# Two spare tiles shift the SBUF addresses of the buffers of a feed-forward stage

## The chip, the cores and the metric

The kernel runs on one core of one Trainium2 chip. The metric is device time in microseconds (us) of one execution, smaller being better. The kernel before takes 998.57 us, the median of three runs between 998.44 and 998.62 us. Nothing but the kernel's program differs between before and after: the inputs, the core and the way of timing are the same.

The engines have short names here: PE is TensorE (matmuls), PEld its loading of weights, DVE is VectorE, ACT is ScalarE, POOL is GpSimd and SP is SyncE, which issues most of the DMAs. SBUF is the on-chip memory, in which a tile has the same address in each of 128 partitions; PSUM is the memory into which matmuls write. All addresses below are bytes within a partition.

## The reference

An input x of 2048 rows by 640 columns goes through two halves. In the first, x is normalized, scaled and convolved along the 2048 rows with a long filter for every column, which the kernel does by its own two-step Fourier transform. In the second, the result is normalized again and goes through a gated feed-forward network of width 1728:

```
h = layernorm(x) * (1 + cb) + sb
gate, up = h @ w1, h @ w3                 # 2048x640 by 640x1728, twice
out = x + gb * ((silu(gate) * up) @ w2)   # 2048x1728 by 1728x640
```

The six row vectors such as cb, sb and gb come from one more small product. All inputs and outputs are 32-bit floats.

## The kernel before, in words

The program has two stages, one after the other on the same core.

**The Fourier stage** takes the time up to some 390 us. Its work is a list of tasks which a planner (the class Plan) puts into one order by written-out ranks; each engine then runs its instructions in just that order (the class InOrder). Its tiles lie in the pools early, gp, tbl and gw, which grow upward from the low end of SBUF, and in xsp, inv and core, which lie against the high end.

**The feed-forward stage** takes the rest. The function change() inside run() (L914) closes the low pools and opens in their place xp, ip and wp; after the plan has been run, run() closes inv and core and opens in their place the pool ffn against the high end (L958). Then ffn() (L755) loops over four blocks b of 512 rows, and within each over 14 slices m of 128 of the 1728 features (the last slice has 64, for gate and up together). One pass of that loop does the following.

- weights_load() (L703) brings the slices of w1, w3 and w2 into the tiles wr and w2r by DMAs of 320 KB. Each is split into a high and a low part, whose sum is the number itself: wh and w2h are copies in the type float32r on ACT (L732, L733), wl and w2l are the differences on DVE (L741, L745).
- up() (L792) multiplies. For each of gate and up, and each of the five blocks k of 128 columns, three matmuls follow one another (L800, L801, L802): high by high, high weights by low activations, low weights by high activations. The weights (128 columns of a tile, 512 bytes in a partition) are loaded into the array; the activations xh or xl (512 columns, 2048 bytes in a partition) move through it. That is 30 matmuls for a full slice.
- gate() (L805) makes the product of silu(gate) and up on ACT and DVE and splits it into ah and al.
- down() (L829) multiplies by w2, again in three matmuls for each of five pieces of the output, 15 in a full slice, all at L837. For pieces k = 0 to 3 the roles are changed: 128 columns of ah or al are loaded as weights and 512 columns of w2h or w2l move. For k = 4, which is done first, w2h or w2l is loaded and ah or al moves, as in up().

The order here is that of the text, with the down() of one slice behind the up() of the next, as the framework's own scheduler arranges it. ln2() (L669) normalizes the next block of 512 rows while the loop runs and writes xh and xl; output() (L839) adds the result to x2 and stores it. During block 0 the last part of the Fourier transform back is still done between the slices (inverse_unit, L660). awake() (L523) puts in a few matmuls of 32-bit floats, with no use of their result, while PE would wait before the first block.

Every matmul of up() and down() works in float32r; all other matmuls (awake, the transposes of ln2 at L691, the Fourier transforms) work in plain 32-bit floats.

The addresses follow from the sizes of the tiles, since a pool puts one tile behind the other. The pool xp begins at 19872, which is 38 times 512 plus 416; nearly all sizes in xp, ip and wp are multiples of 512 (the two small ones, of 480 and 32 bytes, make one together), so that wd, x20, the iz tiles, wr, w2r, wh, w2h, wl and w2l all begin 416 bytes past a multiple of 512. The pool ffn ends at 229344 and begins at 113984, and its tiles xn, xh, xl, v, th, a, ah, al, u, gb, oc and og begin 480 bytes past a multiple of 512; its first three, x21, x22 and x23, begin 320 bytes past one, because five small tiles of 32 bytes follow them. Between the low and the high pools 4512 bytes are free.

Of the kernel before, what the change touches and what calls it, by code (L numbers as in the profile page):

```python
# [10 lines left out]
F32 = mybir.dt.float32  # L11
# [7 lines left out]
P = 128  # L19
# [263 lines left out]
class K:  # L283
# [581 lines left out]
    def run(self):  # L865
# [7 lines left out]
        def open_(name, side=None, bufs=1, space=None):  # L873
            scopes[name] = ExitStack()
            return self.pool(name, bufs=bufs, space=space, ctx=scopes[name], side=side)

        def close(*names):
            for n in names:
                scopes.pop(n).close()
# [34 lines left out]
        def change():  # L914
            close("gw", "tbl", "gp", "early")
            self.xp, self.ip, self.wp = open_("xp"), open_("ip"), open_("wp")
            self.wd = self.xp.tile([P, NJ, 2, 64], F32, name="wd")
            self.x2 = [self.xp.tile([P, 4, D], F32, name="x20")]
            nc.sync.behind = nc.tensor.prev
            self.load_x2(0)  # L920
            nc.sync.dma_start(self.wd, self.t_wd)
            nc.sync.behind = None
            self.stats = self.ln_begin(self.ip, "n0")
        add = plan.add
        add("change", None, 0, change, [f"g{b}.7.p", f"g{b}.7.d"] + [f"h{b}.{i}.x" for i in range(4)], 0)
        add("fx", "SP", 0, None, ["change"], 0, dma=[327680] * 4 + [1048576])
        self.ahead = {}
# [30 lines left out]
        pool = open_("ffn", "right")  # L958
# [20 lines left out]
                nxt[b + 1] = self.ln2(b + 1, pool, ps)  # L979

        self.ffn(nxt, wp, pool, ps, po, mid)
        close("ps", "po", "ffn", "wp", "ip", "xp")

    def mod_cols(self, pm):
# [583 lines left out]
```

## Time and profile before

| what | value |
|---|---|
| median of three timed runs | 998.57 us |
| lowest and highest of them | 998.44 and 998.62 us |
| span of the profiled execution | 994.1 us |
| PE busy in the span | 894.6 us, 90% |
| DVE busy | 665.9 us, 67% |
| ACT busy | 496.7 us, 50% |
| POOL busy | 287.9 us, 29% |

The profile is of one execution. Its span runs from the first to the last instruction; what lies around the span belongs to the execution as well. The profile gives no time of its own for that one execution beside the span; against the median of the timed runs 4.5 us lie around it. Busy time of an engine is the time covered by at least one of its instructions: matmuls overlap in the pipeline, so a PE that is always busy still may be slower or faster at what it does, and the distance from the start of one matmul to the start of the next tells more than the duration of one.

### The profile page before, as it was taken

To read this page: it belongs to the slowest core of one execution; us is meant where nothing else is said; L and a number is where in the kernel's file an instruction comes from. 1 tells how busy PE (TensorE), PEld (TensorE's weight loads), DVE (VectorE), ACT (ScalarE), POOL (GpSimd) and SP (SyncE) were. 2 spreads that over 40 slices of the span, in tenths; PEclk is the share of its full clock that TensorE was granted. 3 is DMA by queue.
4 is the path that set the end of the run, shared out by engine and by line. 5 is a ranking of instruction groups with operands and counts; after the bars stand their busy time and mean duration, and the time that the engine had idled before them with its cause. 6 is when DMAs were issued, how large, how long until landed. Compare 5 with 4: busy or idle time off the path is not lost.

```text
span 994.1 us, 20194 instructions
## 1 busy us (share of the span) xinstructions
PE 894.6 (90%) x8095; PEld 708.9 (71%) x8095; DVE 665.9 (67%) x1235; ACT 496.7 (50%) x829; POOL 287.9 (29%) x293
## 2 busy tenths in 40 slices
PE   1464878889999997999999999999999999999997
PEld 1133766767787863677788888888888888888885
DVE  7998999999999574677564553463644544645443
ACT  6878787979788732432253333343432332433221
POOL 1798798989998330100000000000000000000000
PEclk9986998999999999999999999999999999999999
DMA  9955553614041397996232363332443323543311
GB/s 218 269 184 185 116 135 104 148 52 122 24 108 46 77 272 202 232 233 163 70 90 79 106 162 91 90 98 78 120 132 107 92 80 94 145 119 80 105 28 53
DMA packets 141189, 122.03 MB, mean 123 GB/s; under 512 B 13480, under 2 KB 124840, under 8 KB 139688
## 3 DMA queue, kind: packets, MB, share of 16 engines
q1 hardware_dynamic: 140360, 119.84, 45.8%
q8 instruction: 63, 1.03, 0.5%
q10 hardware_dynamic: 736, 0.92, 0.3%
q14 instruction: 30, 0.25, 0.1%
HBM read 99.75 MB, written 20.97 MB: 121 GB/s over the span
## 4 chain that ended last, share of the span: by engine, by line
PE 72%; DVE 15%; ACT 4%; issue 3%; DMA 3%; POOL 2%; SPq 2%; DVEq 0%; ACTq 0%; POOLq 0%
PE acc L837 19%; PE gu L802 13%; PE gu L801 12%; PE gu L800 12%; PE ps L157 4%; DVE yy L157 3%; PE kps L157 2%; PE fz L157 2%; DVE fp L157 2%; DVE hn L157 2%; PE fk L157 2%; DVE xx L157 2%; PE fh L157 2%; SPq L157 2%; PE iy L652 1%
## 5 line engine op out<-in xcount | busy, mean ns | idle before, releaser
L802 PE MATMUL gu<-xh,wl 128*128 128x512 f32 x540 | 212.9, 394 | 0.0
L801 PE MATMUL gu<-xl,wh 128*128 128x512 f32 x540 | 211.6, 392 | 0.0
L800 PE MATMUL gu<-xh,wh 128*128 128x512 f32 x540 | 210.5, 392 | 0.7 <-ACT xh L666 0.7
L732 ACT ACTIVATE wh<-wr 128x640 fp32r<-128x640 f32 x105 | 71.8, 731 | 136.0 <-PE gu L801 132.8
L744 POOL MEMSET w2l<- 64x640 f32 x3 | 1.9, 628 | 450.6 <-PE acc L837 450.6
L801 PEld LDWEIGHTS gu<-xl,wh 128*128 128x128 f32 x540 | 101.5, 188 | 23.7 <-DVE xl L667 0.2
L800 PEld LDWEIGHTS gu<-xh,wh 128*128 128x128 f32 x540 | 101.4, 188 | 23.2 <-ACT xh L666 1.0
L802 PEld LDWEIGHTS gu<-xh,wl 128*128 128x128 f32 x540 | 101.5, 188 | 21.4
L813 ACT ACTIVATE th<-gu 128x512 f32<-128x512 f32 x52 | 31.1, 599 | 129.8 <-PE gu L802 129.7
L815 DVE TENSOR_TENSOR a<-a,gu 128x512 f32<-128x512 f32 x52 | 35.7, 687 | 87.7 <-PE gu L802 87.5
L157 POOL TENSOR_TENSOR yy<-e,e 128x512 f32<-128x512 f32 x80 | 86.2, 1094 | 17.1 <-PE kps L157 12.2
L814 DVE SCALAR_TENSOR_TENSOR a<-th,gu 128x512 f32<-128x512 f32 x52 | 35.6, 686 | 76.4 <-ACT th L813 76.3
L837 PE MATMUL acc<-w2l,ah 128*128 128x512 f32 x219 | 86.6, 396 | 0.0
L733 ACT ACTIVATE w2h<-w2r 128x640 fp32r<-128x640 f32 x54 | 39.9, 738 | 93.6 <-issue 54.8
L837 PE MATMUL acc<-w2h,ah 128*128 128x512 f32 x219 | 86.6, 395 | 0.0
L741 DVE TENSOR_TENSOR wl<-wr,wh 128x640 fp32r<-128x640 f32 x105 | 82.4, 817 | 0.0
L745 DVE TENSOR_TENSOR w2l<-w2r,w2h 128x640 fp32r<-128x640 f32 (+1 forms) x54 | 44.4, 821 | 56.7 <-ACT w2h L733 56.6
L157 POOL TENSOR_TENSOR ph<-p,p 128x1024 int32<-128x1024 int32 x40 | 80.0, 2000 | 5.2 <-ACT tr L157 5.0
L837 PE MATMUL acc<-w2h,al 128*128 128x512 f32 x203 | 77.2, 395 | 0.0
L157 DVE TENSOR_TENSOR yy<-yy,tr 128x512 f32<-128x512 f32 (+1 forms) x80 | 75.3, 943 | 0.9 <-ACT tr L157 0.6
L157 PE MATMUL kps<-yy,xx 128*32 128x64 f32 x2560 | 53.0, 240 | 24.8 <-DVE xx L157 21.7
L157 PEld LDWEIGHTS kps<-yy,xx 128*32 128x32 f32 x2560 | 46.5, 120 | 34.6 <-issue 17.6
(231 smaller groups left out, 1695.7 us busy)
## 6 DMA issues: line engine op xcount, KB each, us to landing
wr<-in_w SPq DMA_DIRECT2D x104, 320.0 KB, 3.9
w2r<-in_w SPq DMA_DIRECT2D x52, 320.0 KB, 2.9
zd<-zt SPq DMA_DIRECT2D x39, 256.0 KB, 2.8
iz<-zd SPq DMA_DIRECT2D x24, 320.0 KB, 7.2
xs<-in_x SPq DMA_DIRECT2D x16, 320.0 KB, 11.3
hs<-hb SPq DMA_DIRECT2D x20, 256.0 KB, 2.5
xb<-hs SPq DMA_DIRECT2D x20, 256.0 KB, 4.6
x<-in_x SPq DMA_DIRECT2D x16, 320.0 KB, 9.6
```

The lines of the kernel that those rows point to most:

```text
L157: self.prev = self.k.order(f(*a, **kw), self.prev)
L732: self.nc.scalar.activation(wh[:, i], raw[:, i], AF.Copy)
L733: self.nc.scalar.activation(w2h, w2r, AF.Copy)
L741: eng.tensor_tensor(wl[:, i], raw[:, i], wh[:, i].bitcast(F32), op=ALU.subtract)
L745: eng.tensor_tensor(w2l[q], w2r[q], w2h[q].bitcast(F32), op=ALU.subtract)
L800: nc.tensor.matmul(pg, wh[:, k, :], xh[:, k, :], start=(k == 0), stop=False)
L801: nc.tensor.matmul(pg, wh[:, k, :], xl[:, k, :], start=False, stop=False)
L802: nc.tensor.matmul(pg, wl[:, k, :], xh[:, k, :], start=False, stop=(k == KT - 1))
L813: nc.scalar.activation(th, gu[0], AF.Tanh, scale=0.5)
L814: nc.vector.scalar_tensor_tensor(a, th, 1.0, gu[0], op0=ALU.add, op1=ALU.mult)
L815: nc.vector.tensor_mul(a, a, gu[1])
L837: nc.tensor.matmul(acc[k], *two(a, w), start=(m == 0 and i == 0), stop=(m == 12 and i == 2))
```

## The change

Two tiles that no instruction reads or writes are put into two pools.

```diff
         def change():
             close("gw", "tbl", "gp", "early")
             self.xp, self.ip, self.wp = open_("xp"), open_("ip"), open_("wp")
+            self.xp.tile([P, 24], F32, name="pad_left")
             self.wd = self.xp.tile([P, NJ, 2, 64], F32, name="wd")
             self.x2 = [self.xp.tile([P, 4, D], F32, name="x20")]
...
         self.ffn(nxt, wp, pool, ps, po, mid)
+        pool.tile([P, 120], F32, name="pad_right")
         close("ps", "po", "ffn", "wp", "ip", "xp")
```

pad_left has 24 numbers, 96 bytes, and stands first in xp: all that follows in xp, ip and wp begins 96 bytes higher. pad_right has 120 numbers, 480 bytes, and stands last in ffn, a pool whose end is fixed: all else in ffn begins 480 bytes lower. Worked out from the sizes:

| tiles | begin before, past a multiple of 512 | begin after |
|---|---|---|
| wd, x20, iz, wr, w2r, wh, w2h, wl, w2l | 416 | 0 |
| xn, xh, xl, v, th, a, ah, al, u, gb, oc, og | 480 | 0 |
| x21, x22, x23 | 320 | 352 |

The Fourier stage's own tiles stay where they are. No instruction is added, removed or moved in the text of the program.

## The prediction

> **What bounds the kernel now.** I first read the page for the engine that ends last, then the table by stage for the part in which the change lies, then the groups of matmuls, and last the single start times.
>
> ```profile
> span 994.1 us, 20194 instructions
> PE 894.6 (90%) x8095; PEld 708.9 (71%) x8095; DVE 665.9 (67%) x1235; ACT 496.7 (50%) x829; POOL 287.9 (29%) x293
> ...
> PE 72%; DVE 15%; ACT 4%; issue 3%; DMA 3%; POOL 2%; SPq 2%; DVEq 0%; ACTq 0%; POOLq 0%
> PE acc L837 19%; PE gu L802 13%; PE gu L801 12%; PE gu L800 12%; PE ps L157 4%; DVE yy L157 3%; PE kps L157 2%; PE fz L157 2%; DVE fp L157 2%; DVE hn L157 2%; PE fk L157 2%; DVE xx L157 2%; PE fh L157 2%; SPq L157 2%; PE iy L652 1%
> ```
>
> The chain that ended last is PE for 72%, and four lines of the feed-forward stage (L800, L801, L802, L837) are 56% of the span. By stretches of that stage (columns: stretch, its length, then busy us and count of PE, PEld, DVE, ACT and POOL, the granted clock, the share of the DMA engines, GB/s):
>
> ```profile
> 500.00:600.00 100.00, 100.00 (x452) 81.94 (x451) 52.59 (x79) 36.83 (x58) 0.63 (x1) 1.00 0.41 109
> 600.00:700.00 100.00, 100.00 (x446) 81.83 (x445) 48.22 (x70) 35.84 (x55) 0.00 (x0) 1.00 0.33 90
> 700.00:800.00 100.00, 100.00 (x448) 81.77 (x447) 52.82 (x76) 35.34 (x55) 0.63 (x1) 1.00 0.41 111
> 800.00:900.00 100.00, 100.00 (x438) 81.47 (x437) 54.20 (x79) 34.81 (x54) 0.63 (x1) 1.00 0.39 106
> 900.00:980.00 80.00, 80.00 (x349) 65.26 (x348) 33.64 (x48) 22.68 (x35) 0.00 (x0) 1.00 0.24 66
> ```
>
> PE is busy without a gap at full clock; DVE has at most 54%, ACT 37%, the DMA engines 41%. PE's own waits from 400 to 980 us are two:
>
> ```profile
> PE iy L652 <- DVE x L655: 0.4, 1, 0.4
> PE acc L837 <- ACT ah L666: 0.3, 1, 0.3
> ```
>
> So the stage lasts as long as its matmuls do back to back. Faster DMAs, DVE or ACT would buy nothing; the change can act on the end only through the pace of the matmuls.
>
> **What sets that pace.** The groups of the stage (busy us, mean ns of one):
>
> ```profile
> L802 PE MATMUL gu<-xh,wl 128*128 128x512 f32 x540 | 212.9, 394 | 0.0
> L801 PE MATMUL gu<-xl,wh 128*128 128x512 f32 x540 | 211.6, 392 | 0.0
> L800 PE MATMUL gu<-xh,wh 128*128 128x512 f32 x540 | 210.5, 392 | 0.7 <-ACT xh L666 0.7
> L837 PE MATMUL acc<-w2l,ah 128*128 128x512 f32 x219 | 86.6, 396 | 0.0
> L837 PE MATMUL acc<-w2h,ah 128*128 128x512 f32 x219 | 86.6, 395 | 0.0
> L837 PE MATMUL acc<-w2h,al 128*128 128x512 f32 x203 | 77.2, 395 | 0.0
> L837 PE MATMUL acc<-ah,w2h 128*128 128x512 f32 x55 | 22.5, 409 | 0.3 <-ACT ah L666 0.3
> L837 PE MATMUL acc<-ah,w2l 128*128 128x512 f32 x55 | 21.6, 392 | 0.0
> L837 PE MATMUL acc<-al,w2h 128*128 128x512 f32 x51 | 20.3, 398 | 0.0
> ```
>
> In a name the moving operand stands first. That makes 1620 + 161 = 1781 matmuls whose moving operand is a tile of the pool ffn (480 bytes past a multiple of 512) with weights from wp (416), and 641 with the roles changed; eighteen more at the end have another line and are left out. The 392 to 398 ns overlap; the pace is in the start times (start us, duration us):
>
> ```profile
> 652.00 0.39 PE L800 MATMUL gu<-xh,wh 128*128 128x512 f32 x1
> ...
> 664.36 0.39 PE L837 MATMUL acc<-ah,w2h 128*128 128x512 f32 x1
> ...
> 665.05 0.39 PE L837 MATMUL acc<-w2h,ah 128*128 128x512 f32 x1
> ...
> 667.85 0.39 PE L800 MATMUL gu<-xh,wh 128*128 128x512 f32 x1
> ...
> 862.76 0.40 PE L800 MATMUL gu<-xh,wh 128*128 128x512 f32 x1
> ...
> 869.76 0.40 PE L800 MATMUL gu<-xh,wh 128*128 128x512 f32 x1
> ```
>
> 54 matmuls of up() from 652.00 to 664.36 take 12.36 us, 228.9 ns each. The 12 of down() with the roles changed, 665.05 to 667.85, take 233.3 each. There are also stretches of up() at 233.3: 30 from 862.76 to 869.76 in 7.00 us. What would the moving of 512 columns alone cost? The matmuls in plain 32-bit floats tell:
>
> ```profile
> 377.79 7.13 PE L157 MATMUL awake<-wd,ident 128*128 128x512 f32 x16
> ...
> 388.49 2.84 PE L157 MATMUL awake<-wd,ident 128*128 128x512 f32 x6
> ...
> 644.92 1.47 PE L691 MATMUL tp<-ident,xn 128*128 128x128 f32 x12
> ```
>
> ```profile
> L691 PE MATMUL tp<-ident,xn x80: 271/272/329, 394.0 to 793.8; 128*128 128x128 f32 x80
> ```
>
> The row by itself gives min, median and max of one transpose, 271, 272 and 329 ns. The awake groups give (7.13 - 2.84) / 10 = 429 ns from start to start, the transposes (1.47 - 0.27) / 11 = 109 ns. Between 128 and 512 columns that is 0.833 ns a column and 2.4 ns for each instruction, and neither pays anything for its addresses, though wd begins 416 and xn 480 bytes past a multiple of 512. The float32r matmuls take about half as long a column: at 0.417 ns, 512 columns and 2.4 ns would be 215.7. They are 13.2 ns (up) and 17.6 ns (down) over that.
>
> In which steps? Sixteen columns are 64 bytes and take 6.67 ns. 228.9 / 6.67 is 34.3 and 233.3 / 6.67 is 35.0, while 429 / 6.67 is 64.4, which is just its 1024 column times and 2.4 ns. So in the fast type alone the pace falls on whole and third parts of the time for 64 bytes, which speaks for operands that are fetched in pieces of 64 bytes with nothing to spare. All of these operands begin 32 bytes past a multiple of 64. A moving operand of 2048 bytes that begins there touches 33 such pieces instead of 32, a weight tile of 512 bytes 9 instead of 8. And 228.9 against 233.3, with the same shape and the same order of three, goes with which tile moves: k = 4 of down(), whose roles are those of up(), takes (665.05 - 664.36) / 3 = 230. So the place of the operands, or their distance from one another, matters already now.
>
> **The change part by part.** The pads are touched by no instruction: no instruction, DMA or wait is added in the text, and the high and low pools, 4512 bytes apart, still don't meet (96 + 480 bytes). What may change is three things.
>
> First, which old tile lies under a new one, and so which last use the new tile waits for. By the sizes I find the low pools over the same tiles as before, but for the 96 bytes at their start. On the high side x22 and x23 each come free of one tile of the pool inv, four of the small tiles of ln2 lie over another of its output buffers, and og0 over one more tile of core. All of these owners are done before the first inverse product of the second stage, which reads what they stored, and og0 is written only when the first block is done: I take nothing, and both ends of the price are nothing.
>
> Second, DVE, ACT and the DMAs get other addresses. The scaling of ln2 reads x20 (416) in two of its eight DVE instructions and x21 to x23 (320, a multiple of 64) in six:
>
> ```profile
> L680 DVE TENSOR_SCALAR xn<-x,rs_y_n,rs_n_n x8: 605/608/612, 392.9 to 653.1; 128x640 f32<-128x640 f32 x8
> ```
>
> 605 to 612 ns over all eight: no effect of 64 bytes there. That x21 to x23 themselves come to lie 32 bytes past a multiple of 64 should then cost nothing. The DMAs' share has no bearing, since PE waits for none of them from 400 us on; if PE were 6% faster, DVE would rise to 58%, still no bound.
>
> Third, the matmuls. No row here has a float32r operand on a multiple of 64 bytes, so the price is bounded from both sides. Best, all of the excess goes: 1781 x 13.2 ns + 641 x 17.6 ns = 34.8 us. Worst by the rows here, all take the slower pace that is seen: 1781 x 4.4 ns = 7.8 us more. I take one piece of 64 bytes less for each moving operand, 2422 x 6.67 ns = **16.2 us less**. It lies between the bounds and is the row's own step; the other part of the excess would stay with the loading of the weights. All of it is on the path, since PE ends the stage.
>
> [...]
>
> **The rivals.** *All the excess goes*: place was its only cause, and the pace becomes 215.7. For it: plain matmuls show none. Against it: they run at half the pace and may hide anything, the loading of the weights included. 998.6 - 34.8 = 963.8.
>
> *The change does nothing to the pace*: the step is one of time, from the loading of weights beside a moving operand that has no slack, wherever both lie. For it: the same operands of up() run at 228.9 and at 233.3, so history matters. 998.6.
>
> *Slower*: now weights and moving operand begin at the same place within 512 bytes, where they were 64 bytes apart. If the two streams, read at the same time, come to the same part of the memory, up() falls to the pace of down(), and with it everything: 998.6 + 7.8 = 1006.4. It decides as soon as up() loses its 228.9, in the first slice of block 0. For it: turning the distance around, as down() does, costs 4.4 ns already. [...]
>
> *The change doesn't do what it says*: x21 to x23 stay off, but no matmul reads them; the operands of all 2422 do come to multiples of 512.
>
> **How the numbers follow.** The span of the profiled execution is 994.1 us, the median of the timed runs 998.57, and the 4.5 us around the span stay, so that the sum may be taken from the median. One piece less: 998.6 - 16.2 = **982.4 us**, chance 0.38, with an own range of 976 to 991 (1.4 times that to half of it). All gone, 963.8: 0.15. Nothing, 998.6: 0.25. Slower, 1006.4: 0.22. Cases of both signs hold much of the chance, so the range takes both bounds: **963 to 1007**. 0.2% is 2 us, about what a measurement of this kernel can tell from no change: faster 0.53, same 0.25, slower 0.22.
>
> **What would show it.** Up to 390 us the new trace should agree with the old in all its stretches. Then L800 to L802 should start 222 ns apart and the matmuls of down() 227, with mean durations 6 to 7 ns lower in every group above, while the awake matmuls stay at 429, the weight loads stay as they are, and L680 stays within 605 to 612. If the groups move by 13 to 18 ns, all of the excess was place; if up() is at 233, the distance of the two streams is what counts; if neither moves, the step is time alone. I would be wrong altogether if the difference came from before 390 us, from a new wait of PE, or from a clock under 1.00 in the stretches above.

## The result, and the profile after

The changed kernel takes 987.23 us, the median of four runs between 986.33 and 988.79 us; the kernel before takes 998.51 us beside it. The ratio is 0.9887, with an interval of 0.9873 to 0.9901: faster by 11.3 us or 1.1%. The prediction was 982.4, with a range of 963 to 1007. The profiled execution of the changed kernel took 987.09 us, with a span of 985.3, so 1.8 us lie around the span.

The head of the page and its chain of waits, for the changed kernel:

```profile
span 985.3 us, 20196 instructions
PE 884.0 (90%) x8095; PEld 707.7 (72%) x8095; DVE 665.6 (68%) x1235; ACT 496.6 (50%) x829; POOL 287.9 (29%) x293
...
PE 70%; DVE 15%; ACT 4%; DMA 3%; issue 3%; SPq 2%; POOL 2%; DVEq 0%; ACTq 0%; POOLq 0%
PE acc L837 19%; PE gu L800 12%; PE gu L801 12%; PE gu L802 12%; DVE yy L157 3%; PE ps L157 3%; PE kps L157 2%; SPq L157 2%; DVE fp L157 2%; PE fz L157 2%; DVE hn L157 2%; DVE xx L157 2%; PE fk L157 2%; PE fh L157 2%; PE iy L652 1%
```

The same engine and the same four lines carry the end. PE has as many matmuls as before and 10.6 us less busy time; the other engines have what they had. By stretches (the columns are those of the table shown before):

```profile
500.00:600.00 100.00, 100.00 (x457) 83.19 (x456) 54.81 (x82) 38.38 (x60) 0.63 (x1) 1.00 0.39 109
600.00:700.00 100.00, 100.00 (x453) 83.08 (x452) 47.29 (x68) 34.54 (x53) 0.00 (x0) 1.00 0.34 96
700.00:800.00 100.00, 100.00 (x454) 83.04 (x453) 54.82 (x79) 37.22 (x58) 0.63 (x1) 1.00 0.39 109
800.00:900.00 100.00, 100.00 (x444) 82.84 (x443) 52.86 (x78) 33.90 (x53) 0.63 (x1) 1.00 0.40 112
```

PE stays busy without a gap, at the same full clock, and gets more matmuls into the same time: 457, 453, 454 and 444 where there were 452, 446, 448 and 438, 1.3% more. DVE and the DMA engines have as much room as before. The groups of the matmuls (busy us, mean ns of one):

```profile
L800 PE MATMUL gu<-xh,wh 128*128 128x512 f32 x540 | 210.8, 392 | 0.1
L802 PE MATMUL gu<-xh,wl 128*128 128x512 f32 x540 | 210.3, 390 | 0.0
L801 PE MATMUL gu<-xl,wh 128*128 128x512 f32 x540 | 210.3, 390 | 0.0
...
L837 PE MATMUL acc<-w2h,ah 128*128 128x512 f32 x219 | 85.4, 390 | 0.0
L837 PE MATMUL acc<-w2l,ah 128*128 128x512 f32 x219 | 85.4, 390 | 0.0
...
L837 PE MATMUL acc<-w2h,al 128*128 128x512 f32 x203 | 76.1, 390 | 0.0
```

The groups with w2h and w2l moving lose 5 to 6 ns of mean duration, L801 and L802 lose 2 to 4, L800 nothing. The start times say it better (start us, duration us):

```profile
600.75 0.39 PE L800 MATMUL gu<-xh,wh 128*128 128x512 f32 x1
...
607.55 0.39 PE L837 MATMUL acc<-ah,w2h 128*128 128x512 f32 x1
...
608.23 0.39 PE L837 MATMUL acc<-w2h,ah 128*128 128x512 f32 x1
...
610.95 0.39 PE L800 MATMUL gu<-xh,wh 128*128 128x512 f32 x1
```

The 30 matmuls of up() from 600.75 to 607.55 start 226.7 ns apart, and so do the 12 of down() from 608.23 to 610.95. Taken over the whole stage, from start to start where one matmul follows the other directly, the distances are:

| ns from start to start | before | after |
|---|---|---|
| up(), 1606 and 1605 distances | 229.6 | 226.8 |
| down(), k = 4, 152 distances | 229.3 | 227.0 |
| down(), k = 0 to 3, 639 distances | 233.2 | 227.3 |
| all, 2397 and 2396 distances | 230.57 | 226.96 |

The distance is counted for the matmul that it follows. So 3.61 ns for each of some 2400 matmuls, 8.7 us, came from the pace. How long the stage lasts is in the rows of L800, whose first and last start stand behind the durations (min, median, max in ns). The kernel before:

```profile
L800 PE MATMUL gu<-xh,wh x540: 388/388/496, 397.1 to 979.2; 128*128 128x512 f32 x180
```

The changed kernel:

```profile
L800 PE MATMUL gu<-xh,wh x540: 388/389/793, 396.5 to 970.5; 128*128 128x512 f32 x180
```

From the first to the last it was 582.1 us and is 574.0: 8.1 us less. The remaining 3 us of the 11.3 are not in this stage; the last experiments come back to them.

### The profile page after: what moved, and what is told of

The parts are those of the page before. It is cut to its first block, busy times and chain, and to the rows that moved or that the text cites. A ratio compares the mean times of both kernels' runs of the same rounds, so it can differ in the third digit from the quotient of the medians.

```text
span 985.3 us, 20196 instructions
## 1 busy us (share of the span) xinstructions
PE 884.0 (90%) x8095; PEld 707.7 (72%) x8095; DVE 665.6 (68%) x1235; ACT 496.6 (50%) x829; POOL 287.9 (29%) x293
## 4 chain that ended last, share of the span: by engine, by line
PE 70%; DVE 15%; ACT 4%; DMA 3%; issue 3%; SPq 2%; POOL 2%; DVEq 0%; ACTq 0%; POOLq 0%
PE acc L837 19%; PE gu L800 12%; PE gu L801 12%; PE gu L802 12%; DVE yy L157 3%; PE ps L157 3%; PE kps L157 2%; SPq L157 2%; DVE fp L157 2%; PE fz L157 2%; DVE hn L157 2%; DVE xx L157 2%; PE fk L157 2%; PE fh L157 2%; PE iy L652 1%
## 5 line engine op out<-in xcount | busy, mean ns | idle before, releaser
L800 PE MATMUL gu<-xh,wh 128*128 128x512 f32 x540 | 210.8, 392 | 0.1
L802 PE MATMUL gu<-xh,wl 128*128 128x512 f32 x540 | 210.3, 390 | 0.0
L801 PE MATMUL gu<-xl,wh 128*128 128x512 f32 x540 | 210.3, 390 | 0.0
L800 PEld LDWEIGHTS gu<-xh,wh 128*128 128x128 f32 x540 | 101.7, 189 | 21.3 <-ACT xh L666 0.5
L802 PEld LDWEIGHTS gu<-xh,wl 128*128 128x128 f32 x540 | 101.4, 188 | 21.2
L801 PEld LDWEIGHTS gu<-xl,wh 128*128 128x128 f32 x540 | 101.6, 188 | 20.8
```

The costliest lines, as they stand in the source:

```text
L800: nc.tensor.matmul(pg, wh[:, k, :], xh[:, k, :], start=(k == 0), stop=False)
L801: nc.tensor.matmul(pg, wh[:, k, :], xl[:, k, :], start=False, stop=False)
L802: nc.tensor.matmul(pg, wl[:, k, :], xh[:, k, :], start=False, stop=(k == KT - 1))
```

## The experiments

Three theories were set against each other. **A**, that of the prediction: a moving operand that begins off a multiple of 64 bytes pays for one piece more. **B**: the weights pay for it. **C**: only the distance between the places of the weights and of the moving operand counts, so that two streams which are read side by side hinder each other at some distances and not at others; this is the thought behind the rival "slower", but with the sign open.

### The pace alone

A kernel of nothing but bursts of 30 matmuls each, with operands at chosen places; it computes nothing of the reference. Its main line, with m and w the bytes past a multiple of 512 of the moving operand and of the weights:

```diff
+                x = nc.tensor.matmul(acc[i % 2][:c, :n], b[:, j % 5, w // 4:w // 4 + c], a[:, j % 3, m // 4:m // 4 + n],
+                                     start=(j == 0), stop=(j == REPS - 1))
```

> This kernel computes nothing of the reference: it is a row of bursts of 30 float32r matmuls each, back to back, with the moving operand and the weights at chosen distances past a multiple of 512 bytes, and nothing else running. With both at 0 every theory expects the 226.7 ns (34 times the 6.67 ns of 16 columns) of the changed kernel. Theory A, the moving operand pays for one more piece of 64 bytes: off by 32 with weights at 0 gives 233.3, weights off with moving at 0 gives 226.7. Theory B, the weights pay: the other way round, 226.7 and 233.3. Theory C, only the distance between the two counts: 32 and 32, or 416 and 416, give 226.7 as 0 and 0 do, and distances of 64 to 256 at multiples of 64 differ from 0. Under A and B all multiples of 64 give 226.7. If the two beats over 32 belong to the loading of 128 columns of weights, 64 columns of weights give 220 or less and 256 columns moved give 120 (18 beats); plain 32-bit floats give 429 at either place.

A stretch out of some of its bursts (start, length, count). In order, (moving, weights) is (0, 0); (480, 416), as up() had them before; (416, 480), as down() had them; (0, 32); (32, 32); (416, 416); (0, 256):

```profile
28.57 5.15 PE L42 MATMUL acc<-mr,wr 128*128 128x512 f32 x22
...
35.41 5.20 PE L42 MATMUL acc<-mr,wr 128*128 128x512 f32 x22
...
42.30 5.06 PE L42 MATMUL acc<-mr,wr 128*128 128x512 f32 x21
...
49.29 5.06 PE L42 MATMUL acc<-mr,wr 128*128 128x512 f32 x21
...
63.25 5.15 PE L42 MATMUL acc<-mr,wr 128*128 128x512 f32 x22
...
76.87 5.15 PE L42 MATMUL acc<-mr,wr 128*128 128x512 f32 x22
...
146.51 5.15 PE L42 MATMUL acc<-mr,wr 128*128 128x512 f32 x22
...
315.58 5.31 PE L42 MATMUL acc<-mf,wf 128*128 128x512 f32 x12
```

A length covers all starts and the last duration, so (5.15 - 0.39) / 21 = 226.7 ns is the pace at (0, 0), and it is the same at (32, 32), (416, 416) and (0, 256). (480, 416) gives (5.20 - 0.39) / 21 = 229.0, (416, 480) and (0, 32) give (5.06 - 0.39) / 20 = 233.5: the two paces of the kernel before, without anything of the kernel around them. The last row is of plain 32-bit floats at (0, 0): eleven steps of 429 ns, as in the kernel, and 0.59 us for the last record itself. A step is not a whole matmul here: the trace has 120 records for the 60 plain matmuls of this kernel, two for each, so that one takes 858 ns. A float32r matmul has one record, 1350 for the 1350 of this kernel.

A and B fall here. (32, 32) is off a multiple of 64 on both sides and pays nothing, with the 226.7 ns of (0, 0), while (0, 32) and (32, 0) pay 6.6 to 6.8 ns with one side on it. C had (0, 256) among the distances that pay, and it doesn't; from here on C is the distance modulo 256. Equal places at multiples of 32 give 226.67 ns, which is 34.0 times the 6.67 ns of 16 columns, and no pair gives less. Some expectations on the size of the operands failed: 64 columns of weights instead of 128 gave 229.9, not 220 or less, so that loading less does not make a moving operand of 512 columns faster, though the loading itself took 134 ns instead of 190 on the mean. With fewer columns moved, equal places gave 173.3 at 384 and 120.0 at 256, (226.67 - 120.0) / 256 = 0.417 ns a column and 13.3 ns besides, for each instruction. At 480 columns, no multiple of 128, it is 216.6, some 3 ns more than that line.

### One pad without the other

```diff
+            self.xp.tile([P, 24], F32, name="pad_left")
```

> Weights of up() at 0 and its moving operand still at 480; in down() for k = 0 to 3 the weights at 480 and the moving operand at 0. Theory A (the moving operand pays): up() stays at 229 to 233, down() goes from 233.3 to 226.7, 641 x 6.6 ns = 4 us less than before, ratio 0.996. Theory B (the weights pay): up() goes to 226.7, down() stays at 233.3, 1781 x 2.2 ns = 4 us less, ratio 0.996; the two differ in which group moves. Theory C (the distance alone): 480 against 0 is a distance of 32 bytes, not met so far; both orders keep an excess over 226.7.

1001.78 us, ratio 1.0042 (1.0023 to 1.0061): slower, up() at 233.2 and down() at 233.0. The other one:

```diff
+        pool.tile([P, 120], F32, name="pad_right")
```

> The moving operand of up() at 0 and its weights still at 416; in down() for k = 0 to 3 the moving operand at 416 and the weights at 0. Theory A (the moving operand pays): up() goes to 226.7 and down() stays at 233.3, 4 us less than before, ratio 0.996. Theory B (the weights pay): up() stays at 229 to 233, down() goes to 226.7, also 4 us less. Theory C (the distance alone): 96 bytes apart; both orders keep an excess.

1004.93 us, ratio 1.0065 (1.0045 to 1.0085): slower, up() at 233.5 and down() at 233.3. One row for each, the whole stretch from 400 to 970 us with its matmuls behind PE's busy time. The kernel before:

```profile
400.00:970.00 570.00, 569.28 (x2533) 456.10 (x2532) 307.13 (x536) 195.39 (x302) 2.67 (x4) 1.00 0.43 112
```

The left pad alone:

```profile
400.00:970.00 570.00, 568.76 (x2506) 450.92 (x2507) 307.30 (x534) 196.28 (x304) 4.48 (x5) 1.00 0.42 113
```

The right pad alone:

```profile
400.00:970.00 570.00, 568.77 (x2506) 450.83 (x2505) 306.47 (x534) 194.55 (x302) 3.18 (x4) 1.00 0.42 112
```

Either pad costs 27 matmuls of 2533 in the same time, where both together gain 37. Each pad brings one of the two operands to multiples of 512, and by A as by B both should have been faster, at 0.996. What each does is to change the distance, from 64 bytes to one that is worse for up(), 233.2 and 233.5 ns where it had 229.6, and up() has most of the matmuls.

### Equal places that are no multiples of 512

Three kernels ask how much of "multiples of 512" is needed. First, 32 bytes on each side, so that all of these operands begin at 448:

```diff
+            self.xp.tile([P, 8], F32, name="pad_left")
...
+        pool.tile([P, 8], F32, name="pad_right")
```

> Pads of 32 bytes on either side, so that weights and moving operands begin 448 bytes past a multiple of 512: on a multiple of 64, not of 128. If 64 bytes is the piece that counts (A, B, and C too, since the distance is 0), all matmuls run at 226.7 and the time is that of the change, ratio 0.988 to 0.990. If multiples of 128 or more are needed, up() and down() stay at 229 and 233 and the ratio is 1.000.

988.71 us, ratio 0.9898 (0.986 to 0.9936), up() at 226.8 and down() at 227.1. Second, 64 bytes on the right only, so that both begin at 416, which is no multiple of 64:

```diff
+        pool.tile([P, 16], F32, name="pad_right")
```

> One pad of 64 bytes on the high side, none on the low side: weights and moving operands of the feed-forward stage all begin 416 bytes past a multiple of 512, so none begins at a multiple of 64, as before the change, but the two are equal. Theory C (equal places): all groups at 226.7 ns, the stage 8 to 9 us shorter, ratio 0.989 to 0.992, the same as the change. Any theory of alignment by itself (multiples of 64 or 512): up() and down() stay at 229 and 233, ratio 1.000.

988.35 us, ratio 0.9901 (0.9883 to 0.9919). Third, both pads as in the change, but the right one 256 bytes shorter, so that weights begin at 0 and moving operands at 256:

```diff
+            self.xp.tile([P, 24], F32, name="pad_left")
...
+        pool.tile([P, 56], F32, name="pad_right")
```

> Weights at multiples of 512, moving operands 256 bytes past one (in down() for k = 0 to 3 the other way round). If the two streams share a part that repeats every 256 bytes, this is equal to the change: 226.7 ns, ratio 0.989 to 0.992. If it repeats only every 512, an excess of 2 to 7 ns stays and the ratio is 0.995 to 1.005.

987.89 us, ratio 0.989 (0.9868 to 0.9912). In the same stretch, with both at 416:

```profile
400.00:970.00 570.00, 568.73 (x2569) 462.69 (x2569) 311.10 (x540) 198.71 (x308) 4.45 (x5) 1.00 0.43 113
```

With the operands 256 apart:

```profile
400.00:970.00 570.00, 568.73 (x2571) 462.61 (x2570) 308.67 (x538) 195.97 (x304) 1.89 (x3) 1.00 0.41 111
```

And with the change itself:

```profile
400.00:970.00 570.00, 568.76 (x2570) 462.97 (x2569) 309.40 (x538) 197.10 (x305) 2.07 (x4) 1.00 0.41 112
```

2569, 2571 and 2570 matmuls are one result. One pad of 64 bytes does what the two of 96 and 480 bytes do, and no operand needs to lie at a multiple of 64 for it, as 0.9901 with all of them at 416 shows.

### All distances

The bursts again, 16 matmuls each, for all places at steps of 16 bytes below 256, in two orders; this computes nothing of the reference either. Its list of cases:

```diff
+GRID = [(m, w, 512, 128, "r") for m in range(0, 256, 16) for w in range(0, 256, 16)]
+CASES = [(0, 0, 512, 128, "r")] * 3 + GRID
+CASES += [GRID[i * 97 % 256] for i in range(256)]
```

> Computes nothing of the reference: bursts of 16 float32r matmuls for all 256 pairs of places of moving operand and weights at multiples of 16 bytes within 256, once in order and once in another order, then 508 and fewer columns, then bfloat16. Theory C, narrowed by the first row of bursts (the two streams share a part of the memory that repeats every 256 bytes): 226.7 on the whole diagonal of equal places at multiples of 32, 229 to 237 off it, in both orders. Theory A or B (multiples of 64): 226.7 at 0, 64, 128 and 192 whatever the other operand does, which the first row has all but excluded. If a pair lies under 226.7, a kernel faster than the change can be built. In bfloat16 the operands are half as long; theory C expects little or no excess over 215.7 there at any place.

Rows of three bursts, with the moving operand at 32 and the weights at 32, 64 and 224, and one in bfloat16:

```profile
149.87 2.88 PE L47 MATMUL acc<-mr,wr 128*128 128x512 f32 x12
...
157.16 2.73 PE L47 MATMUL acc<-mr,wr 128*128 128x512 f32 x11
...
194.39 2.68 PE L47 MATMUL acc<-mr,wr 128*128 128x512 f32 x11
...
1941.70 2.75 PE L47 MATMUL acc<-mb,wb 128*128 128x512 bf16 x12
```

(2.88 - 0.39) / 11 is 226, (2.73 - 0.39) / 10 is 234 and (2.68 - 0.39) / 10 is 229. Over all places that are multiples of 32, what counts is the place of the weights less that of the moving operand, modulo 256 (the mean of the last 7 distances of each burst, both orders):

| distance, bytes | 0 | 32 | 64 | 96 | 128 | 160 | 192 | 224 |
|---|---|---|---|---|---|---|---|---|
| mean ns from start to start | 226.9 | 233.6 | 233.1 | 234.3 | 233.1 | 233.6 | 229.3 | 233.3 |

Before the change up() stood at 416 - 480 = -64, which is 192 in the table, and down() at 64. That is why the same two tiles gave 229.6 in one role and 233.2 in the other. Moving both places by the same multiple of 32 bytes changes nothing that the bursts show: 226.7 at (0, 0), (32, 32) and (416, 416).

Two things limit the table. The pace of a pair isn't there from its first matmul on. In the second order the burst before always has other places, and then equal places reach the floor only after about nine matmuls. With both at 32, the first nine and the last six:

```profile
1333.78 2.25 PE L47 MATMUL acc<-mr,wr 128*128 128x512 f32 x9
...
1336.09 1.52 PE L47 MATMUL acc<-mr,wr 128*128 128x512 f32 x6
```

That is (2.25 - 0.39) / 8 = 232 ns first and (1.52 - 0.39) / 5 = 226 then. At 192, moreover, the pace has two values. One of the sixteen bursts there stayed at 233.3, the others at 228.4 to 229.3; and in the kernel before five runs of up(), 114 matmuls in all, among them the 30 that the prediction shows from 862.76 on, went at 233.3 as well, the same five in both profiles of it. What decides between the two isn't shown. In the changed kernel no run of up() goes at 233.3.

And at odd multiples of 16 the table does not hold. Equal places are not the floor there: rows of both at 16, and of the moving operand at 16 with the weights at 48:

```profile
86.13 3.63 PE L47 MATMUL acc<-mr,wr 128*128 128x512 f32 x15
...
93.79 3.33 PE L47 MATMUL acc<-mr,wr 128*128 128x512 f32 x14
```

(3.63 - 0.39) / 14 is 231 and (3.33 - 0.39) / 13 is 226. All eight equal pairs at odd multiples of 16 have 231 to 233 ns, and all pairs with both at odd multiples of 16 and a distance of 32 or of 192 have the floor, in both orders. Some other pairs with one operand at an odd multiple of 16, or both, differ by up to 10 ns between the two orders, so that the bursts before them matter. No operand of the kernel's float32r matmuls lies at such a place. No pair is under 226.57. In bfloat16 the pace is 215.9 at 512 columns (the row gives (2.75 - 0.38) / 11 = 215) and 109.1 at 256, and the place had no effect at the four pairs of 0 and 32 that were run.

### The distance turned around

64 bytes on each side: the weights of up() come to 480 and its moving operand to 416, just what down() had, and the other way round.

```diff
+            self.xp.tile([P, 16], F32, name="pad_left")
...
+        pool.tile([P, 16], F32, name="pad_right")
```

> A left and a right spare tile of 64 bytes each: the weights wp then begin at 480 and the moving ffn buffers at 416 of 512, so the two operands of up() and down() change places against the kernel before. If the distance between weights and moving operand modulo 256 bytes sets the pace (theory C), the paces of the two groups change places too: up() and down() k=4 go from about 229 to 233.3 ns, down() k=0-3 from 233.3 to about 229; 1781 x 4.4 - 641 x 4.3 ns = +5 us, ratio about 1.005. If what counts is which of the two places a moving operand or a weight has by itself (theories A and B), nothing of the kind: both stay off multiples of 64 as before, ratio 1.000.

1002.62 us, ratio 1.0052 (1.0032 to 1.0072), where C had 1.005. up() went to 233.3 and k = 4 to 233.1 as expected. down() with k = 0 to 3 went to 231.2 instead of 229, so it gained half of what the table says; its runs are of 12 matmuls at most, about as many as the bursts above took to settle, but that this is the reason isn't shown. The whole mean is 232.72 ns. The stage in the same stretch as above, 22 matmuls fewer than the 2533 of the kernel before:

```profile
400.00:970.00 570.00, 569.22 (x2511) 452.04 (x2510) 307.05 (x535) 195.69 (x302) 3.33 (x5) 1.00 0.43 113
```

### Which of the streams meet

In the changed kernel the weights of one matmul are loaded while the one before runs: the L801 that starts at 600.98 us has its weights loaded from 600.75 on, in 0.19 us, and 600.75 is the start of the L800 before it. So the streams that meet may be those of two matmuls, and these bursts let even and odd matmuls read different places:

```diff
+for d in (32, 64, 96, 128, 192):
+    PAIRS += [((0, 0), (d, d)), ((0, d), (d, 0))]
```

> Bursts of 30 float32r matmuls, each with its own loading of 128 columns of weights, computing nothing of the reference. Within a burst even and odd matmuls read two different places: d bytes past a multiple of 512 for both operands of every second matmul and 0 for both of the others (pairs equal within each matmul), or moving at 0 with weights at d and moving at d with weights at 0 in turn (pairs equal between one matmul's moving operand and the next one's weights). If what collides is a matmul's moving operand with the weights of the next one, which are loaded beside it, the second kind has the floor of 226.7 ns for every d and the first kind pays (about 233 for 32, 64, 96 and 128). If it is the two operands of one matmul that count, the first kind has the floor and the second pays. If the places count by their history alone, neither kind has the floor.

Rows of four bursts: both operands at 0 throughout; moving 0 and weights 32 throughout; (0, 0) and (32, 32) in turn; (0, 32) and (32, 0) in turn:

```profile
21.34 5.15 PE L39 MATMUL acc<-mr,wr 128*128 128x512 f32 x22
...
35.02 5.06 PE L39 MATMUL acc<-mr,wr 128*128 128x512 f32 x21
...
49.01 5.02 PE L39 MATMUL acc<-mr,wr 128*128 128x512 f32 x21
...
55.95 5.22 PE L39 MATMUL acc<-mr,wr 128*128 128x512 f32 x22
```

That is 226.7, 233.5, 231.5 and 230.0 ns. Neither kind of change in turn has the floor, at no d; the paces lie between 228.3 and 234.0. So which two streams hinder each other stays open: it is not the pair of one matmul alone, nor only one matmul's moving operand with the next one's weights. What was shown is that, at multiples of 32, the floor comes where all operands that follow one another agree modulo 256.

### The same kernels again

The change a second and a third time, and the kernel before against itself, to see what else moves.

> The change itself, unaltered, beside the kernels of this call, for the size of its gain. The pace of its matmuls fell from 230.6 to 226.9 ns from start to start over 2396 of them, 8.7 us, so 0.9913 is expected; 0.989 and less would mean that some 2 us come from elsewhere, such as the Fourier stage.

986.68 us, ratio 0.988 (0.986 to 0.9899); up() at 226.8, down() at 227.2. The pace repeats. The 0.9913 that it gives by itself lies outside this interval, so by this run some of the gain comes from elsewhere.

> The kernel before, unchanged, against itself: ratio 1.000 by every theory, and a second profile of it. up() at 229.6 and down() k=0-3 at 233.2 ns again; the first matmul of the feed-forward part anywhere between 395 and 400 us. How far its first stage and its time wander shows how much of a difference of 2 to 3 us between two kernels is no effect of either.

997.09 us, ratio 0.9996 (0.9982 to 1.001); up() at 229.6, down() at 233.3. Its stage:

```profile
L800 PE MATMUL gu<-xh,wh x540: 388/388/503, 401.7 to 983.8; 128*128 128x512 f32 x180
```

The same 582.1 us as in the first profile of it, but it starts 4.6 us later. The first stage of one and the same program wanders by that much, and the second stage repeats.

> The changed kernel a third time, beside the kernel before. The feed-forward stage was 8.2 us shorter in every profile of a kernel with equal places, which by itself is a ratio of 0.992; the timed runs gave 0.988 to 0.990. If the 2 us between them are the wandering of the first stage, this run lies nearer to 0.992 than the two before; if something of the first stage is shorter too, it lies at 0.988 to 0.990 again.

986.26 us, ratio 0.9863 (0.9843 to 0.9882). Its stage:

```profile
L800 PE MATMUL gu<-xh,wh x540: 387/389/499, 398.4 to 971.8; 128*128 128x512 f32 x180
```

573.4 us, 8.7 less than before. At 0.9863 this run is not nearer to 0.992 than the two before it, but farther off, and below the 0.988 to 0.990 of the other case too. By what was expected, this speaks against mere wandering of the first stage; but the kernel before, at 999.68 us, was also slower beside this run than beside any other. In all six kernel runs with equal places the median is 9 to 13 us lower than that of the kernel before beside it, and 8 to 9 of these are the pace. In single profiles the first stage ended at 397.1 and 401.7 us before, and at 396.5, 399.7 and 398.4 after, which doesn't separate the two, and what follows the last L800 takes 14.8 to 14.9 us in all five. Where the rest comes from, 0.5 to 5 us, is not settled: it is within the wandering of one execution, but all six medians lean the same way.

## Why the prediction was right, and where it failed

**What bounds the kernel: right.** In the feed-forward stage only the pace of the matmuls changed, PE stayed busy, and the gain of pace came off the end: 8.7 us by the distances, 8.1 us by the length of the stage. Some 3 us of the 11.3 lie outside that stage; the prediction has no term for them, and the runs don't explain them.

**Faster, for operands that come to better places: right in sign, and wrong in the reason.** The step of the prediction that failed is "I take one piece of 64 bytes less for each moving operand". A moving operand at 32 past a multiple of 64 pays nothing when the weights are there too, 226.7 ns at (32, 32), and the left or right pad alone made the kernel slower, at 1.0042 and 1.0065. What counted is the distance of the two streams modulo 256, which the prediction named ("So the place of the operands, or their distance from one another, matters already now") and then gave to the rival. So the sign was luck: pads that bring both operands to multiples of 512 also bring them to equal places, and only the second of these counts: with all at 416 the ratio is 0.9901.

**16.2 us: nearly twice too much.** For down() the size happened to be right, 233.2 to 227.3, 6.0 ns of the 6.67. For up() and k = 4, three quarters of the matmuls, it was 2.8 of 6.67, since 229.6 was already close to the floor. 1757 x 2.8 + 639 x 6.0 = 8.8 us. The whole gain of 11.3 us is nearer to 16.2 only by the part that nothing explains.

**The rival "slower" had its premise the wrong way round.** It took the same place within 512 bytes for the slow one. Among multiples of 32 it has the fastest pace of the eight distances: 226.9 against 229 to 234. Read to the end, the rows of before show a pace that depends on the sign of the distance, 229.6 at -64 and 233.2 at +64, which no count of 64-byte pieces gives.

**All the excess goes: no.** 215.7 ns is the pace of bfloat16, measured at 215.9. In float32r at least 13.2 ns of each instruction stay, at every place and with any number of weight columns that was run: no pair is under 226.57, and 512 columns at 0.4167 are 213.3. The way to 215.7 was not sound either: the prediction takes the 429 ns of the awake records for the time of a matmul, and they are half of one, since awake() issues 8 and 3 matmuls where the trace has 16 and 6 records. By the matmul, float32r takes a quarter as long a column as plain floats, not half: 0.417 ns against 858 / 512 = 1.68.

**The signs.** The awake matmuls and the scaling of ln2, in the changed kernel:

```profile
375.90 7.13 PE L157 MATMUL awake<-wd,ident 128*128 128x512 f32 x16
...
387.62 2.84 PE L157 MATMUL awake<-wd,ident 128*128 128x512 f32 x6
```

```profile
L680 DVE TENSOR_SCALAR xn<-x,rs_y_n,rs_n_n x8: 603/610/614, 392.1 to 649.7; 128x640 f32<-128x640 f32 x8
```

(7.13 - 2.84) / 10 is 429 ns again, though wd has moved against ident, and 603 to 614 ns is as good as 605 to 612: right. 227 ns for down(): right, 227.0 and 227.3. 222 ns for L800 to L802: wrong, 226.8. Mean durations 6 to 7 ns lower in every group: wrong, they are lower by 0 to 6. Its readings for the rivals, "13 to 18 ns" and "up() is at 233", did not come either. PE has one wait more, of 0.5 us, too short to matter. Whether the first 390 us agree can't be read from single profiles, since two of the kernel before differ by 4.6 us there.

**The 4.5 us around the span: wrong.** They are 1.8, in the changed kernel and in the second profile of the one before (998.7 and 1000.53). The first profile of before, with 994.1, was then of an execution some 2.6 us faster than its median. This cost the prediction nothing, since it took the sum from the median.

## What to carry to other kernels

Where PE runs float32r matmuls back to back, read the distances between their starts, and put weights and moving operands at multiples of 32 bytes that agree modulo 256 in all groups that follow one another: here that was 226.9 ns where the other distances had 229 to 234, and one spare tile of 64 bytes a partition was worth 1.0%. A pad that aligned one of the two alone cost 0.4 and 0.7%, so both go together. When the two roles of the same two tiles run at different paces, as up() at 229.6 ns and down() at 233.2 did here, look at the distance and its sign before the alignment of either.

## What the runs showed of the hardware

- float32r, 128 columns of weights: 226.7 ns for 512 columns moved, 173.3 for 384, 120.0 for 256, at equal places; 0.417 ns a column and 13.3 ns an instruction, and some 3 ns more at 480. bfloat16: 215.9 for 512 and 109.1 for 256. Plain 32-bit floats, 512 columns: 858 for a matmul, in two records of 429.
- At other distances of weights and moving operand, 229 to 234 ns for float32r with both at multiples of 32; 0 and 256 bytes have the same pace, 226.7 in the bursts and a ratio of 0.989 in the kernel, and a pace is not the same for a distance and its opposite (64: 233.1, -64: 229.3, in some stretches 233.3).
- With both at odd multiples of 16, equal places gave 231 to 233 ns, and distances of 32 and 192 the floor of 226.7.
- After other places, equal ones took about nine matmuls to come to the floor.
- Fewer columns of weights, 32, 64 or 96, made 512 columns slower, 229.5 to 231.7, and not faster.
